# Pacing the loads of an opening stage: at most three on the way

## The chip, the cores and the metric

The kernel runs on one core of a Trainium2 chip. The metric is the time of one execution on the device in microseconds (us); lower is better. Before the change it is 587.9 us, the median of three runs (587.0 to 588.2).

## The reference

Two blocks follow each other. The first is a retention block: for each of 4 batches and 8 heads a 64 by 64 state decays by a factor of the head at each of 768 steps and takes in an outer product of k and v; the output at a step is q times the state. The second is a feed-forward layer on the result.

```python
for t in range(S):                      # S = 768; B, H, D = 4, 8, 64
    state = gamma[None, :, None, None] * state + np.einsum('bhd,bhe->bhde', k[:, :, t], v[:, :, t])
    y[:, :, t] = scale * np.einsum('bhd,bhde->bhe', q[:, :, t], state)
x = y.transpose(0, 2, 1, 3).reshape(B * S, H * D)      # 3072 x 512
h = x @ w_in                                           # 512 x 2048
g = h * (1.0 / (1.0 + np.exp(-h)))
out = g @ w_out                                        # 2048 x 512
```

The weights w_in and w_out come as 64-bit floating point, everything else as 32-bit.

## The kernel before

The sequence is cut into chunks of 128 steps, 6 for each batch. A pair of a chunk and a batch is a *unit*; there are 24, counted chunk by chunk (units 0 to 3 are the four batches of chunk 0). For a unit the kernel

- loads its k, q and v, 256 KB each (`load`, one DMA of 1024 runs of 256 bytes, issued by SyncE),
- transposes k and q on PE (`T`, or `TK` and `TQ` apart) and copies them out of PSUM with ACT,
- scales k and q on DVE by the decay (`K`, `Q`; `KA` does it on ACT),
- makes the scores and the state's increments on PE (`SC`, which reads k, v and the transposes), masks them on DVE (`A`),
- makes the unit's y on PE (`YS`, `Y0`, `YB`) and splits it into three parts for the exact products with w_in (`X`).

The weights are converted from 64 bits and split in the same way. A *slice* of w_in is 128 of its 2048 columns: `load_w` brings it in three DMAs, one of 256 KB and two of 128 KB, into one of two buffers (`wf`), and ACT and DVE convert and split it in small steps (`W`). When a chunk's y is there, PE multiplies it with the slices (`PP`, `PH`, and `product_in` later); g goes to DRAM and comes back for the product with w_out, which fills the second half of the kernel.

The order of the work up to the first products is **written out by hand** for all engines, SyncE's DMA issues among them: a long list of calls at the end of the function, from `load("k", 0)` down to `begin_w()`, closed by `early_order.close()`. After that only PE's order is written; the other engines, SyncE too, are placed by the scheduler. SyncE issues in order, so an issue that waits holds all later ones. What an issue waits for before the change is a free buffer (for a load into a buffer that was used before) and, for the DMA lanes, of which there are eight, the landing of the eighth DMA ahead of it.

`hold(done)` writes a SyncE instruction that does nothing but wait until the instruction `done` is complete, for a DMA until it has landed. Before the change nothing calls it.

Of the kernel before, what the change touches and what calls it, by code (L numbers as in the profile page):

```python
# [35 lines left out]
def kernel(  # L36
# [28 lines left out]
    nc = tc.nc  # L65
    B, H, S, D = q.shape
    DM, DF = moe_w_in.shape
    C = 128
# [64 lines left out]
    def split_w(*of):  # L133
        steps = split_steps(*of)
        next(steps)
        yield
        list(steps)
# [15 lines left out]
    early, last = {}, []  # L153

    def load(name, n):
        if n >= len(units):
            return
        c, b = units[n]
        src = {"k": k, "q": q, "v": v}[name]
        if n == 4 * B and name == "k":  # L160
            t = conv.tile([128, H, D], FP32, tag="wl", name=f"kf_{n}")
            nc.sync.dma_start(out=t, in_=src[b, :, ds(c * C, C)].rearrange("h t d -> t h d"))
            kqv[name][n] = t
            return
        if n < EARLY:

            if n not in early:
                early[n] = wpool.tile([128, 3, H, D], FP32, tag=f"w{4 + n}", name=f"kqv_{n}")
            t = early[n][:, "kqv".index(name)]
        else:  # L170
            t = ld.tile([128, H, D], FP32, tag=f"{name}f", name=f"{name}f_{n}",
                        bufs=2 if name == "q" else 3)
        nc.sync.dma_start(out=t, in_=src[b, :, ds(c * C, C)].rearrange("h t d -> t h d"))  # L173
        kqv[name][n] = t

    staged = {}

    def load_w(i):
        if i >= 2 * NF:
            return
        if wide:
            t = stage.tile([128, 2 * DM], U32, tag="wf", name=f"wf_{i}")
            w_in, w_out, n = moe_w_in.bitcast(U32), moe_w_out.bitcast(U32), 256
        else:
            t = stage.tile([128, DM], FP32, tag="wf", name=f"wf_{i}")
            w_in, w_out, n = moe_w_in, moe_w_out, 128
        if i < NF:  # L190
            to = t.rearrange("p (i o f) -> o p i f", o=2, f=n)
            src = w_in[:, ts(i, n)].rearrange("(i o p) f -> o p i f", o=2, p=128)
            last[:] = [nc.sync.dma_start(out=to[0], in_=src[0]).ins]
            for j in range(2):
                nc.sync.dma_start(out=to[1, ts(j, D)], in_=src[1, ts(1 - j, D)])
        else:
            nc.sync.dma_start(out=t, in_=w_out[ts(i - NF, 128), :])
        staged[i] = t
# [35 lines left out]
    def convert_w(i):  # L234

        if patient[0]:
            waiting.append(i + W_AHEAD)
        elif i + W_AHEAD not in staged:
            load_w(i + W_AHEAD)
        out = []  # L240
        steps = convert_steps(i, out)
        for _ in range(6):
            next(steps, None)

        def rounded():
            list(steps)
            return out[0]

        return rounded

    def early_slice(i):

        out = []
        yield from convert_steps(i, out)
        yield
        steps = split_steps(i, out[0], "wi", w_sb, None)
        next(steps)
        yield from steps
# [44 lines left out]
    def begin_w():  # L303

        i = taken[0]
        taken[0] += 1
        split = split_w(i, convert_w(i)(), "wi", w_sb, True)
        next(split)
        half_split.append(split)
# [102 lines left out]
    def hold(done):  # L412

        i = nc.sync.nop().ins
        tc.add_manual_dep(i, done.name, mybir.DependencyInfo(
            mybir.DependencyClass.Sync, mybir.DependencyReason.DATA), reason="hold")
# [276 lines left out]
    def halves(m):  # L693
# [36 lines left out]
        for name in "kqv":  # L730
            for n in (m + 1, m + 2):
                if (n, name) not in apart and EARLY <= n <= LATER and n == (
                        m + 1 if name == "v" or n >= LATER else m + 2):
                    load(name, n)
# [153 lines left out]
    def TQ(n):  # L888
        next(tsteps[n])
# [20 lines left out]
    def W(i, times=1):  # L910
        if i not in slices:
            slices[i] = early_slice(i)
        for _ in range(times):
            next(slices[i], None)

    def loads(n):
        for name in "kqv":
            load(name, n)
# [42 lines left out]
    def KA(n):  # L961
        t = kqv["k"][n]
        for h in range(H):
            nc.scalar.activation(out=t[:, h, :], in_=t[:, h, :], func=AF.Copy,
                                 scale=gk[:, units[n][0], h : h + 1])


    load("k", 0)
    load("q", 0)
    load("v", 0)  # L970
    load_w(0)
    load("k", 1)
    load("q", 1)
# [5 lines left out]
    load("q", 3)  # L979
    load("v", 3)  # L980
    load_w(1)
    load("k", 4)
    load("q", 4)
# [83 lines left out]
    X(3)  # L1067
    TQ(4)
    W(1)
    load("k",6)  # L1070
    W(1)
    load_w(2)
# [129 lines left out]
    Q(8)  # L1202
    load("q",11)
    taken[0] = 3
    begin_w()

    early_order.close()
# [9 lines left out]
    last = ([(c, f) for c in range(2) for f in range(NF - 4, NF)] +  # L1217
            [(2, f) for f in range(half, NF)])
# [84 lines left out]
    def apart_cols(t):  # L1303

        return t.rearrange("p (o n) -> p o n", o=2)

    def unwoven(t):

        return t.rearrange("p (n o) -> p o n", o=2)
# [8 lines left out]
    for c in range(NC):  # L1318
# [9 lines left out]
        for f in range(NF):  # L1328
# [4 lines left out]
            t = ready[n]  # L1333
            if f >= early_f:
                continue
            for b in range(B):
                gh, glo, gm = (t[:, i, ts(b, C)] for i in range(3))
                oa, ob = acc[b]
                for o, g, i in (oa, gh, 0), (oa, glo, 1), (ob, gm, 2):
                    nc.tensor.matmul(o, lhsT=g, rhs=woven(wo[f][:, i, :],  # L1340
                                                          (c, b) == (NC - 1, B - 1)),
                                     start=f == 0 and i != 1,
# [4 lines left out]
        if early_f < NF:  # L1347
# [3 lines left out]
                         for x in ("left", "right")]  # L1351
            nc.scalar.activation(out=apart_cols(halves_of[0]),
                                 in_=unwoven(acc[B - 1][0][:, left]), func=AF.Copy,
# [7 lines left out]
        for b, o, parts, cols in ends:  # L1361
            for f in range(early_f, NF):
                for i in parts:
# [3 lines left out]
                                     start=o is last_left and (f, i) == (early_f, 0),  # L1367
                                     stop=f == NF - 1 and i != 0,
                                     skip_group_check=cols != whole)
        for b in range(B):  # L1370
            oa, ob = acc[b]
            if c == NC - 1 and b == B - 1:
# [4 lines left out]
                for i, (x, cols, op) in enumerate(((last_left, left, ALU.add),  # L1377
                                                   (oa, right, ALU.subtract))):
                    nc.vector.scalar_tensor_tensor(
                        out=apart_cols(o[i]), in0=unwoven(x[:, cols]), scalar=ONE_E,  # L1380
# [44 lines left out]
```

## Time and profile before

| | before |
|---|---|
| median of three runs | 587.9 us |
| profiled execution | 586.4 us |
| its span, first to last instruction | 584.4 us |
| PE busy | 576.4 us, 99% of the span |
| DVE, ACT busy | 399.1 us, 321.7 us |
| DMA, mean over the span | 186 GB/s |

The profile is taken from one execution, which has its own time; the span lies inside that time. PE is the matrix engine, PEld its weight loads, DVE the vector engine, ACT the activation engine, POOL the general one, and SP is SyncE (SPq: its DMA issues). In rows of the timeline the columns are start, duration, engine, line, operation, and the tiles written and read. A row that begins with an engine and has an arrow and a name after it, such as "PE y L576 <- issue", tells who waited for whom: total us, times, longest. A tile view gives, for the instructions chosen, the shortest, median and longest duration in ns, the first and last start, and, for DMA issues, the time from the start of the issue to the landing. Buffer numbers are left out of the names: kqv holds k, q or v of units 0 to 7, kf, qf and vf those of later units, and wf a slice of the weights.

### The profile page before, as it was taken

Reading aid. Unit: us, or ns where it says so; the run is one execution under the profiler, and the core shown is the slowest. Engines: PE = TensorE matmul, PEld = TensorE weight load, DVE = VectorE, ACT = ScalarE, POOL = GpSimd, SP = SyncE. Lnnn points to the kernel's source line nnn. Section 1 sums busy time; section 2 is a strip of 40 time slices with the busy share of each in tenths; the row PEclk is TensorE's granted clock in tenths of the full one; section 3 lists DMA queues with packets and bytes.
Section 4 is the critical chain, followed back from the end, with each engine's and each line's share of the span. In section 5 each row is a group of like instructions: output and inputs, shape, how many; then the busy total and the mean of one; then the engine's idle time right before and its main releaser. Section 6 shows DMA issues by size and latency. Waiting matters only on the chain.

```text
span 584.4 us, 13651 instructions
## 1 busy us (share of the span) xinstructions
PE 576.4 (99%) x5512; PEld 499.9 (86%) x5512; DVE 399.1 (68%) x678; ACT 321.7 (55%) x561; POOL 29.4 (5%) x84
## 2 busy tenths in 40 slices
PE   8999999999999999999999999999999999999997
PEld 6787888888888888888888888888888888888886
DVE  3898998678678876666799994736545563645632
ACT  7657766546356466545566675544544545545311
POOL 3000000100031211210000000000000000000000
PEclk9999999999999999999999999999999999999999
DMA  9998978986489899997589862523524443433301
GB/s 193 215 220 192 218 192 278 267 259 214 145 192 232 234 283 284 255 265 230 171 281 326 288 207 77 195 93 111 178 79 139 144 119 97 165 123 102 115 1 72
DMA packets 144334, 108.89 MB, mean 186 GB/s; under 512 B 101136, under 2 KB 109584, under 8 KB 144272
## 3 DMA queue, kind: packets, MB, share of 16 engines
q1 hardware_dynamic: 144128, 107.90, 66.0%
q8 instruction: 43, 0.70, 0.5%
q14 instruction: 19, 0.16, 0.1%
q10 hardware_dynamic: 144, 0.13, 0.1%
HBM read 66.06 MB, written 36.70 MB: 176 GB/s over the span
## 4 chain that ended last, share of the span: by engine, by line
PE 95%; SPq 2%; DVE 1%; DMA 1%; issue 1%; ACT 0%; DVEq 0%; POOL 0%; POOLq 0%; ACTq 0%
PE ha L757 28%; PE o L1340 21%; PE oa L1340 14%; PE hb L757 14%; PE ob L1340 7%; PE y L576 4%; PE sc L518 2%; PE sc L528 2%; SPq L173 1%; DMA kqv<-in_q_dram 1%; PE ha L928 1%; PE kp L486 1%; PE qp L486 0%; PE o L1364 0%; PE hb L928 0%
## 5 line engine op out<-in xcount | busy, mean ns | idle before, releaser
L757 PE MATMUL ha<-xt,wi 128*128 128x512 f32 x736 | 175.7, 382 | 0.0
L757 PEld LDWEIGHTS ha<-xt,wi 128*128 128x128 f32 x736 | 137.7, 189 | 20.0
L1340 PE MATMUL o<-wo,gs 128*128 128x512 f32 x564 | 137.2, 379 | 0.0
L1340 PEld LDWEIGHTS o<-wo,gs 128*128 128x128 f32 x564 | 106.5, 189 | 15.3 <-DVE o L1389 0.2
L852 DVE TENSOR_TENSOR gs<-gr,gs 128x512 fp32r<-128x512 f32 x96 | 62.0, 684 | 83.0 <-ACT gs L850 83.0
L1340 PE MATMUL oa<-wo,gs 128*128 128x512 f32 x376 | 111.8, 379 | 0.0
L849 ACT ACTIVATE gr<-gr 128x512 f32<-128x512 f32 x96 | 59.7, 629 | 67.8 <-DMA gr<-gd 63.8
L757 PE MATMUL hb<-xt,wi 128*128 128x512 f32 x368 | 94.4, 379 | 0.0
L781 ACT ACTIVATE g<-ha 128x512 f32<-128x512 f32 x87 | 52.1, 599 | 76.5 <-PE ha L757 64.9
L787 DVE SCALAR_TENSOR_TENSOR g<-hb,g 128x512 f32<-128x512 f32 x87 | 59.7, 686 | 40.5 <-ACT g L781 33.6
L1340 PEld LDWEIGHTS oa<-wo,gs 128*128 128x128 f32 x376 | 71.1, 189 | 10.1
L757 PEld LDWEIGHTS hb<-xt,wi 128*128 128x128 f32 x368 | 69.6, 189 | 9.9
L850 ACT ACTIVATE gs<-gr 128x512 fp32r<-128x512 f32 x96 | 53.1, 621 | 38.7 <-PE ob L1340 30.4
L1340 PE MATMUL ob<-wo,gs 128*128 128x512 f32 x188 | 71.3, 379 | 0.0
L853 DVE SCALAR_TENSOR_TENSOR gs<-gs 128x512 fp32r<-128x512 f32 x96 | 61.9, 682 | 0.1
L1340 PEld LDWEIGHTS ob<-wo,gs 128*128 128x128 f32 x188 | 35.5, 189 | 5.1
L212 ACT ACTIVATE ca<-wf 128x512 f32<-128x512 f32 x32 | 27.1, 847 | 15.1 <-DVE cs L225 9.1
L225 DVE SCALAR_TENSOR_TENSOR cs<-ca,cs 128x512 uint32<-128x512 uint32 x32 | 22.1, 690 | 0.8
L536 DVE TENSOR_TENSOR am<-sc,decay 128x512 f32<-128x512 f32 x24 | 16.5, 686 | 8.8 <-PE sc L528 7.7
L576 PE MATMUL y<-qt,mid 64*64 64x64 f32 x376 | 20.0, 220 | 0.9 <-issue 0.9
L657 DVE SCALAR_TENSOR_TENSOR xt<-xt 128x512 fp32r<-128x512 f32 x28 | 19.6, 704 | 0.5
L1389 DVE TENSOR_TENSOR o<-o,o 128x512 f32<-128x512 f32 x10 | 6.6, 687 | 17.8 <-ACT o L1388 17.8
(137 smaller groups left out, 582.9 us busy)
## 6 DMA issues: line engine op xcount, KB each, us to landing
gr<-gd SPq DMA_DIRECT2D x96, 256.0 KB, 2.8
gd<-g SPq DMA_DIRECT2D x87, 256.0 KB, 3.8
wf<-in_moe_w_out_dram SPq DMA_DIRECT2D x16, 512.0 KB, 4.4
out_dram<-o SPq DMA_DIRECT2D x23, 256.0 KB, 2.4
wf<-in_moe_w_in_dram SPq DMA_DIRECT2D x16, 256.0 KB, 4.4
wf<-in_moe_w_in_dram SPq DMA_DIRECT2D x32, 128.0 KB, 4.2
kf<-in_k_dram SPq DMA_DIRECT2D x16, 256.0 KB, 4.6
qf<-in_q_dram SPq DMA_DIRECT2D x16, 256.0 KB, 4.4
```

Source lines behind the costliest of these rows:

```text
L212: top = nc.scalar.activation(out=a.bitcast(FP32), in_=hi.bitcast(FP32), func=AF.Abs, scale=2.0 ** -3).ins
L225: nc.vector.scalar_tensor_tensor(out=s, in0=a, scalar=3, in1=s, op0=ALU.logical_shift_left, op1=ALU.bitwise_xor)
L576: i = nc.tensor.matmul(to[ts(e, D), o, a, :], lhsT=lhsT, rhs=rhs, start=key not in started, stop=True, skip_group_check=True).ins
L657: nc.vector.scalar_tensor_tensor(out=x[2], in0=x[1].bitcast(FP32), scalar=-1.0 / EPS, in1=x[0].bitcast(FP32), op0=ALU.mult, op1=ALU.add)
L757: nc.tensor.matmul(hb if i == 2 else ha, lhsT=w_sb[f][:, i, ts(kk, 128)], rhs=woven(xt[c][:, i, kk, :]), start=kk == 0 and i != 1, stop=kk ...
L781: copied[:] = [nc.scalar.activation(out=to, in_=ha, func=AF.Copy, scale=scale * ONE_E).ins]
L787: taken_out[:] = [nc.vector.scalar_tensor_tensor(out=to, in0=hb, scalar=-scale, in1=to, op0=ALU.mult, op1=ALU.add).ins]
L849: nc.scalar.activation(out=g, in_=g, func=AF.Silu)
L850: nc.scalar.activation(out=t[:, 0, :], in_=g, func=AF.Copy, scale=HALF)
L852: nc.vector.tensor_tensor(out=t[:, 1, :], in0=g, in1=high, op=ALU.subtract)
L853: nc.vector.scalar_tensor_tensor(out=t[:, 2, :], in0=t[:, 1, :].bitcast(FP32), scalar=-1.0 / EPS, in1=high, op0=ALU.mult, op1=ALU.add)
L1340: nc.tensor.matmul(o, lhsT=g, rhs=woven(wo[f][:, i, :], (c, b) == (NC - 1, B - 1)), start=f == 0 and i != 1, stop=f == NF - 1 and i != 0 o ...
```

## The change

From unit 6's k in the written order to the end of that order, SyncE issues a load only when the third load ahead of it has landed. All loads of `load` and the w_in loads of `load_w` go through a new function `paced`, which keeps a list of them and, while `pace[0]` is not zero, calls `hold` on the third last. Pacing is turned on just before `load("k",6)` and off just before `begin_w()`. Each of the three DMAs of a slice counts as a load.

```diff
-        nc.sync.dma_start(out=t, in_=src[b, :, ds(c * C, C)].rearrange("h t d -> t h d"))
+        paced(nc.sync.dma_start, out=t, in_=src[b, :, ds(c * C, C)].rearrange("h t d -> t h d"))
...
+    flying, pace = [], [0]
+
+    def paced(start, **operands):
+        if pace[0] and len(flying) >= pace[0]:
+            hold(flying[-pace[0]])
+        flying.append(start(**operands).ins)
+        return flying[-1]
...
-            last[:] = [nc.sync.dma_start(out=to[0], in_=src[0]).ins]
+            last[:] = [paced(nc.sync.dma_start, out=to[0], in_=src[0])]
             for j in range(2):
-                nc.sync.dma_start(out=to[1, ts(j, D)], in_=src[1, ts(1 - j, D)])
+                paced(nc.sync.dma_start, out=to[1, ts(j, D)], in_=src[1, ts(1 - j, D)])
...
     W(1)
+    pace[0] = 3
     load("k",6)
...
     taken[0] = 3
+    pace[0] = 0
     begin_w()
```

The order of the instructions stays the same on every engine; only what SyncE waits for changes. Before, at the start of the stretch, SyncE's issues and the semaphores that each waits for are these (DMAHW0 to DMAHW7 are the eight lanes; the first rows are q and v of unit 5, then unit 6's k, the third slice's three pieces, unit 6's q, unit 7's k, unit 6's v).

```order
L173 DMA kqv_308<-in_q_dram 128x8x64 [waits DMAHW6_49]
L173 DMA kqv_308<-in_v_dram 128x8x64 [waits DMAHW7_49]
L173 DMA kqv_821<-in_k_dram 128x8x64 [waits DMAHW0_49]
L193 DMA wf_823<-in_moe_w_in_dram 128x2x256 [waits DMAHW1_49,DVE_49,Activation_49]
L195 DMA wf_823<-in_moe_w_in_dram 64x2x256 [waits DMAHW2_49]
L195 DMA wf_823<-in_moe_w_in_dram 64x2x256 [waits DMAHW3_49]
L173 DMA kqv_821<-in_q_dram 128x8x64 [waits DMAHW4_49]
L173 DMA kqv_828<-in_k_dram 128x8x64 [waits DMAHW5_49]
L173 DMA kqv_821<-in_v_dram 128x8x64 [waits DMAHW6_49]
```

Each waits for its own lane, that is for the eighth DMA ahead of it. The same issues after the change:

```order
L181 DMA kqv_308<-in_q_dram 128x8x64 [waits DMAHW6_49]
L181 DMA kqv_308<-in_v_dram 128x8x64 [waits DMAHW7_49]
L181 DMA kqv_821<-in_k_dram 128x8x64 [waits DMAHW5_49,DMAHW0_49]
L181 DMA wf_824<-in_moe_w_in_dram 128x2x256 [waits DVE_49,DMAHW1_49,DMAHW6_49,Activation_49]
L181 DMA wf_824<-in_moe_w_in_dram 64x2x256 [waits DMAHW7_49,DMAHW2_49]
L181 DMA wf_824<-in_moe_w_in_dram 64x2x256 [waits DMAHW0_49,DMAHW3_49]
L181 DMA kqv_821<-in_q_dram 128x8x64 [waits DMAHW1_49,DMAHW4_49]
L181 DMA kqv_833<-in_k_dram 128x8x64 [waits DMAHW2_49,DMAHW5_49]
L181 DMA kqv_821<-in_v_dram 128x8x64 [waits DMAHW3_49,DMAHW6_49]
```

From unit 6's k on each issue waits for one lane more, that of the third load ahead: unit 6's q (lanes 1 and 4) for the slice's main piece, which went out on lane 1, and unit 6's v (lanes 3 and 6) for the slice's last piece on lane 3. 26 issues have such a wait, the last being that of unit 11's q.

## The prediction

> **What bounds the kernel now.** First the page: the span, the share of each engine, and the chain that ended last.
>
> ```profile
> span 584.4 us, 13651 instructions
> PE 576.4 (99%) x5512; PEld 499.9 (86%) x5512; DVE 399.1 (68%) x678; ACT 321.7 (55%) x561; POOL 29.4 (5%) x84
> PE 95%; SPq 2%; DVE 1%; DMA 1%; issue 1%; ACT 0%; DVEq 0%; POOL 0%; POOLq 0%; ACTq 0%
> ```
>
> PE is the bound from end to end: 576.4 of 584.4 us. PE's order is written by hand, and it is the same in both kernels, so a microsecond that PE waits is a microsecond of the end, and a load that lands sooner than PE wants it is worth nothing. The question is therefore how much PE waits in the stretch that the change touches. Next the table by stretches, for the paced stretch (26 to 57 us) and what follows, and the chain, for the last place where it runs through a load.
>
> ```profile
> 26.00:57.00 31.00, 29.66 (x684) 25.16 (x685) 27.16 (x50) 20.70 (x44) 0.36 (x4) 1.00 1.00 217
> 57.00:75.00 18.00, 18.00 (x401) 15.15 (x400) 17.72 (x34) 11.64 (x26) 0.27 (x3) 1.00 0.86 195
> 10.47 4.75 DMA kqv<-in_q_dram
> ```
>
> The columns of the first two rows are the stretch, its length, the busy time of PE, PEld, DVE, ACT and POOL, the granted clock, the DMA share and GB/s. PE idles 31.00 - 29.66 = 1.34 us in the paced stretch and not at all in the next. The clock is 1.00 in both. The last load in the chain is a unit's q that lands at 15.2 us; from there on PE, DVE and ACT set the pace although the DMA engines are full (share 1.00). So the kernel gains nothing by loads that come sooner, and the price of the change is how far it eats into the lead that the loads have over PE.
>
> **What the change does to the queue.** No instruction moves on any engine. Of SyncE's loads, 26 get one more wait: unit 6's k, six q, five more k, five v, and nine pieces of three w_in slices (a slice is a piece of 256 KB and two of 128 KB, and each piece counts as a load). Today SyncE runs ahead as far as the queue takes it:
>
> ```profile
> 26.16 0.82 SPq L173 DMA_DIRECT2D kqv<-in_k_dram  x1
> 27.11 1.21 SPq L193 DMA_DIRECT2D wf<-in_moe_w_in_dram  x1
> 28.37 1.26 SPq L195 DMA_DIRECT2D wf<-in_moe_w_in_dram  x2
> 29.67 0.60 SPq L173 DMA_DIRECT2D kqv<-in_q_dram  x1
> 30.32 1.11 SPq L173 DMA_DIRECT2D kqv<-in_k_dram  x1
> 31.48 2.22 SPq L173 DMA_DIRECT2D kqv<-in_v_dram  x1
> 53.92 0.82 SPq L173 DMA_DIRECT2D qf<-in_q_dram  x1
> ```
>
> These are the issues of unit 6's k, the third w_in slice, unit 6's q, unit 7's k, unit 6's v, and, last of the paced ones, unit 11's q. The tile view in a narrow window gives the landing of a single load, counted from the start of its issue; in the order of the rows: unit 6's k, the slice's main piece, one of its small pieces, unit 6's q, its v, unit 11's q.
>
> ```profile
> L173 SPq DMA_DIRECT2D kqv<-in_k_dram x1: 822/822/822, 26.2 to 26.2; - x1
> DMA to landing us min/median/max: 4.8/4.8/4.8
> ...
> L193 SPq DMA_DIRECT2D wf<-in_moe_w_in_dram x1: 1211/1211/1211, 27.1 to 27.1; - x1
> DMA to landing us min/median/max: 5.9/5.9/5.9
> ...
> L195 SPq DMA_DIRECT2D wf<-in_moe_w_in_dram x1: 609/609/609, 29.0 to 29.0; - x1
> DMA to landing us min/median/max: 5.4/5.4/5.4
> ...
> L173 SPq DMA_DIRECT2D kqv<-in_q_dram x1: 603/603/603, 29.7 to 29.7; - x1
> DMA to landing us min/median/max: 5.5/5.5/5.5
> ...
> L173 SPq DMA_DIRECT2D kqv<-in_v_dram x1: 2221/2221/2221, 31.5 to 31.5; - x1
> DMA to landing us min/median/max: 5.6/5.6/5.6
> ...
> L173 SPq DMA_DIRECT2D qf<-in_q_dram x1: 824/824/824, 53.9 to 53.9; - x1
> DMA to landing us min/median/max: 4.7/4.7/4.7
> ```
>
> Unit 6's k lands at 26.16 + 4.8 = 31.0, unit 11's q, 25 loads later, at 53.92 + 4.7 = 58.6: 27.6 us, or 1.1 us a load. An issue to landing of about 5.3 us at 1.1 us a load means that four to five loads are under way at a time. The change leaves at most three. What three can carry depends on how long one load takes with less before it. The nearest row is a load of the same size later on, with the queue almost empty:
>
> ```profile
> L162 SPq DMA_DIRECT2D kf<-in_k_dram x1: 387/387/387, 156.8 to 156.8; - x1
> DMA to landing us min/median/max: 3.1/3.1/3.1
> ```
>
> With 0.1 us for SyncE to see the landing and start (an estimate: its own gaps between issues in the rows above are 0.04 to 0.13), three loads in 3.1 + 0.1 us are 1.07 us a load, which is what the full queue delivers now, 1.1. That is the lower bound of the new pace. The upper bound is today's 5.3 us to landing: 5.4 / 3 = 1.8 us a load. I take a value near the lower end, about 1.2, because most of today's 5.3 us is time behind the loads ahead, and there will be fewer of them. It is not 1.07 because the six small pieces now hold a place among the three for as long as a whole load, where today they pass in about half its time: 6 times 0.5 us is some 3 us over the stretch.
>
> The Trainium skill, page "DMA: Bandwidth & Descriptors", section "Anatomy of one DMA — SWDGE (gpsimd) path", puts a transfer at 2.0 us and its bytes over 436 GB/s. By that a 256 KB load would take an estimated 2.6 us, three in flight would give 0.9 us a load, and pacing would cost nothing at all; the 3.1 us of the row above are longer, and the measurement decides.
>
> **Where PE meets a late load.** The leads are smallest where pacing begins, just behind the w_in slice. The rows are PE's transposes of unit 6's q, its products with unit 6's v, and the transposes of unit 11's q.
>
> ```profile
> 36.40 0.60 PE L486 MATMUL qp<-ident,kqv 128*128 128x128 f32 x4
> ...
> 38.81 0.34 PE L518 MATMUL sc<-kqv 64*64 64x64 f32 x8
> ...
> 63.38 0.22 PE L496 MATMUL kp<-ident,qf 64*128 64x64 f32 x1
> ```
>
> Unit 6's q lands at 29.67 + 5.5 = 35.2, so it leads by 1.2 us. Now it waits for the third load ahead, the slice's main piece, which lands at 27.11 + 5.9 = 33.0. That piece stands behind the same loads as before, so I keep its landing. The q then starts at 33.1 and lands at the earliest at 33.1 + 3.1 = 36.2, just in time; by today's 5.5 us it would be 38.6, 2.2 us late. Between them I take one other load's 1.1 us in front of it: 37.3, which is 0.9 us late. Unit 6's v waits for the small piece, 29.02 + 5.4 = 34.4 (its issue starts 0.65 us behind the first small piece's). It starts at 34.5, earliest landing 37.6, with two loads in front of it about 39.3, against 38.81: 0.5 late, but PE has already slipped 0.9, so that adds nothing. For unit 11's q, 25 loads at 1.2 us instead of 1.1 put it 2.5 us later, at 61.1 against 63.38: still in time. The slips don't add up, since PE is moved once by the latest of them.
>
> Everything else is covered. The added waits themselves (a SyncE wait instruction takes hundredths of a microsecond) stand where SyncE would wait anyway. Behind the waiting SyncE are only the later loads of the written order, then the next w_in slices and the stores, which are due later still; their cover is the same lead that unit 11's q has, several times the slip. If it were gone, a late w_in slice would stop ACT and DVE, which convert it, for as long as it is late. The sum: -0.1 to +2.2 us, taken as +0.8, the 0.9 less 0.1 for a PE idle moment that falls into the slip.
>
> **The rivals.** (1) Pacing hides entirely: the load takes its unhurried 3.1 us, q lands at 36.2, v at 37.6 or a little behind, and PE never waits. For it: 1.07 against 1.1 us a load. Against: the lead left is 0.2 us at one place. Time: that of before, give or take 0.2.
>
> (2) Faster: with a shorter queue, the short transfers that compete with the loads (instructions for the engines among them) come through sooner and PE's small stops go. These are PE's largest waits from 26 to 64 us (total, times, longest):
>
> ```profile
> PE y L576 <- issue: 0.9, 2, 0.6
> PE sc L518 <- issue: 0.3, 1, 0.3
> PE y L576 <- POOL token L407: 0.3, 1, 0.3
> ```
>
> The two kinds that nothing in the trace explains ("issue") are 1.2 us together. With all of PE's idle time gone the gain is 1.34 us; I take 0.6. The profile does not say that the queue causes these stops. The same page of the Trainium skill, section "Queues, rings and completion order", says that each DMA engine takes turns between the queues that have work, a packet at a time; by that a transfer on another queue doesn't wait behind all loads, a shorter queue would save it little, and this rival would give nothing. No row here shows the turns.
>
> (3) Slower: three in flight don't fill the DMA engines. The mechanism is SyncE's round trip: a landing, then an issue, then the flight. Its place is the far end of the paced stretch, where the lags of 25 loads have added up. The lead of unit 11's q is 63.38 - 58.6 = 4.8 us, so it decides from 27.6 + 4.8 = 32.4 us for 25 loads, 1.3 us a load, an issue to landing of 3.8 us. Halfway between 3.1 and 5.3, at 4.2 us, a load comes every 1.43 us, 25 take 35.8, unit 11's q lands at 66.8 and PE waits 3.4 us there. At 4.0 us to landing it would be 1.8 us, at 4.5 us 5.9. For it: a landing takes as much as 5.9 us here. Against: those were behind four others.
>
> **How the numbers follow.** The profiled execution took 586.4 us, its span 584.4, some 2 us lying outside; the median of the three runs is 587.9, and I add to that. My forecast, a slip of 0.2 to 2.2 us at unit 6, has 0.42 and gives 587.9 + 0.8 = 588.7, at most 590.1. The hidden case has 0.24 (587.9), the faster 0.18 (587.3, at best 586.6), the slower 0.16 (591.3, from 589.7 to 593.8). A measurement of this kernel can tell about 0.2% from no change, 1.2 us. Beyond that lie, on the slow side, all of the last case and some 0.15 of the first, 0.31 together; on the fast side half of the faster case, 0.09; the remaining 0.60 is within. The range 586.6 to 590.8 takes in the bounds of the first three cases and the beginning of the slower one.
>
> **What would show it.** Right: in the profile after, the loads from unit 6's k on take 3.1 to 4.2 us to land, not 5.3; PE or PEld has a new wait of 0.5 to 1 us put down to a load of q or v at 36 to 39 us, and unit 11's q still comes in time. The hidden case shows no such wait and 29.7 us of PE in the same 31. The faster case shows fewer "issue" waits. The slower one shows PE waiting for a load near 58 to 65 us. The forecast is wrong if PE waits more than 2 us for loads, or if the time moves while no wait for a load appears.

## The result and the profile after

The changed kernel takes 589.8 us, the median of nine runs (588.3 to 592.0), against 587.9 us (587.0 to 588.2) before: a ratio of 1.0038, 95% interval 1.0026 to 1.0051. By the ratio it is some 2.2 us slower, by the medians 1.9. The forecast of 588.7 us was too low by about 1 us; the range held. Two executions of the variants below ran at a granted clock of 0.85 and 0.75, the profiled one with four in flight among them, and no time or row here comes from them.

The first rows are the page of the profile after, its span, engines and the chain that ended last; the next two are the same stretches as in the prediction, 26 to 57 and 57 to 75 us, now with pacing.

```profile
span 588.1 us, 13676 instructions
PE 575.9 (98%) x5512; PEld 499.0 (85%) x5512; DVE 400.3 (68%) x678; ACT 321.5 (55%) x561; POOL 28.9 (5%) x84
PE 87%; DMA 7%; SPq 4%; issue 0%; ACT 0%; DVE 0%; DVEq 0%; ACTq 0%
...
26.00:57.00 31.00, 28.34 (x682) 24.17 (x683) 27.01 (x50) 19.99 (x43) 0.35 (x4) 1.00 0.80 183
57.00:75.00 18.00, 17.05 (x394) 14.04 (x393) 16.64 (x32) 11.76 (x26) 0.18 (x2) 1.00 0.90 209
```

PE does the same work (575.9 us) in a longer span. DMA and SyncE had 1% and 2% of the chain and have 7% and 4%. In the paced stretch the DMA engines fell from a share of 1.00 and 217 GB/s to 0.80 and 183: on average a fifth of them now stands idle, while SyncE waits for landings. PE idles 2.7 us there instead of 1.3, and 0.95 us in the next stretch, where it had no idle time. The two profiled spans differ by 3.7 us, more than the medians; 1.3 us of that are two later stalls of PE, which come up again below.

These are PE's waits from 26 to 80 us (total, times, longest):

```profile
PE qp L492 <- DMA kqv<-in_q_dram: 1.1, 1, 1.1
PE sc L524 <- DMA kqv<-in_v_dram: 0.7, 1, 0.7
PE kp L502 <- DMA qf<-in_q_dram: 0.6, 2, 0.4
PE sc L524 <- DVE kqv L430: 0.4, 1, 0.4
PE kp L502 <- DMA kf<-in_k_dram: 0.4, 1, 0.4
...
PE y L582 <- issue: 0.2, 1, 0.2
```

The loads waited for are unit 6's q and v and, behind 57 us, the q of units 10 and 11 and unit 11's k. Together these waits are 2.8 us, where the profile of before had none in this stretch. "issue" is down from 1.2 us to 0.2. It may be that stops which PE had anyway have gone into the waits, but that is not shown: such stops vary from none to 1.5 us in the profiles below. The same three PE rows as in the prediction, now, in the timeline:

```profile
37.50 0.52 PE L492 MATMUL qp<-ident,kqv 128*128 128x128 f32 x3 [1.06 <-DMA kqv<-in_q_dram]
...
40.54 0.35 PE L524 MATMUL sc<-kqv 64*64 64x64 f32 x9 [0.69 <-DMA kqv<-in_v_dram]
...
65.26 0.27 PE L502 MATMUL kp<-ident,qf 64*128 64x64 f32 x1 [0.22 <-DMA qf<-in_q_dram]
```

They were at 36.40, 38.81 and 63.38 us: 1.1, 1.7 and 1.9 us late. How the loads came to be late is read off the chain of waits, in order of time (start, duration, what):

```profile
27.73 4.42 DMA kqv<-in_k_dram
...
32.16 0.02 SPq L420
...
32.21 3.19 DMA wf<-in_moe_w_in_dram
...
35.42 0.02 SPq L420
...
35.47 4.94 DMA kqv<-in_v_dram
...
40.54 0.69 PE sc L524 x32
```

Unit 6's k goes out at 27.73 and takes 4.42 us; L420, the new wait (the line of `hold`), ends 0.03 us after it landed and the slice's last piece starts 0.03 us later; that piece, half as large, takes 3.19 us; then unit 6's v takes 4.94 us, and PE starts on it. Up to PE the chain is nothing but flights, one after the other, with 0.06 to 0.07 us between them.

### The profile page after: what moved, and what is told of

Its sections match the earlier page's. It is cut to its first block, busy times and chain, and to the rows that moved or that the text cites. A ratio compares the mean times of both kernels' runs of the same rounds, so it can differ in the third digit from the quotient of the medians.

```text
span 588.1 us, 13676 instructions
## 1 busy us (share of the span) xinstructions
PE 575.9 (98%) x5512; PEld 499.0 (85%) x5512; DVE 400.3 (68%) x678; ACT 321.5 (55%) x561; POOL 28.9 (5%) x84
## 4 chain that ended last, share of the span: by engine, by line
PE 87%; DMA 7%; SPq 4%; issue 0%; ACT 0%; DVE 0%; DVEq 0%; ACTq 0%
PE ha L763 26%; PE o L1348 21%; PE oa L1348 14%; PE hb L763 12%; PE ob L1348 7%; SPq L181 4%; PE y L582 3%; DMA wf<-in_moe_w_in_dram 2%; DMA kqv<-in_k_dram 2%; PE sc L524 1%; PE sc L534 1%; DMA wf<-in_moe_w_out_dram 1%; DMA kqv<-in_v_dram 1%; DMA qf<-in_q_dram 1%; DMA wr<-wod 1%; DMA vf<-in_v_dram 1%
```

## The experiments

Two explanations stood against each other at first: the supply is limited by the round trip of a load divided by the number in flight; or the wait instructions themselves, or something later in the kernel, cost the time. All runs below are the changed kernel with the edit shown, compared with the kernel before on the same chip. Losses in us are worked out from the ratios; the medians give up to 0.4 us more or less.

**Two in flight.**

```diff
-    pace[0] = 3
+    pace[0] = 2
```

> Pace 2 instead of 3: an issue waits for the second load ahead. Theory (a load's round trip, some 3.1 to 4.3 us from issue to landing in the run with pace 3, divided by the number in flight, sets the supply): two in flight give 1.6 to 2.1 us a load, 25 loads take 40 to 52 us instead of 27.6, the leads of 1.2 to 4.8 us are gone many times over, and the kernel is 8 to 14 us slower than before. Rival A (the added wait instructions are what costs, not what they wait for): same count of waits as with pace 3, so +2 us as there. Rival B (the loss lies later, in stalls near 84 and 324 us that have nothing to do with loads): +2 us as there.

598.3 us against 585.9: ratio 1.0207 (1.0191 to 1.0223), 12.1 us slower. PE's waits for loads from 26 to 80 us, and the issue to landing of the paced loads (the last number, median us):

```profile
PE kp L502 <- DMA qf<-in_q_dram: 5.4, 2, 4.2
PE sc L524 <- DMA kqv<-in_v_dram: 1.9, 2, 1.3
PE qp L492 <- DMA kqv<-in_q_dram: 1.8, 1, 1.8
PE sc L524 <- DMA vf<-in_v_dram: 1.6, 1, 1.6
...
kf<-in_k_dram SPq DMA_DIRECT2D x4, 256.0 KB, 3.3
qf<-in_q_dram SPq DMA_DIRECT2D x4, 256.0 KB, 3.1
wf<-in_moe_w_in_dram SPq DMA_DIRECT2D x6, 128.0 KB, 3.3
```

A single load lands sooner than with three in flight, after 3.0 to 3.5 us by kind, and half a load (128 KB) takes as long as a whole one. Two of them in 3.3 + 0.06 us are 1.7 us a load. The same count of wait instructions cost some six times as much, so it is what they wait for. The waits for loads are 10.7 us of the 12.1. Some of the rest may be the clock: the granted clock from 57 to 75 us was 0.91 in this execution, 1.00 before.

**Four in flight.**

```diff
-    pace[0] = 3
+    pace[0] = 4
```

> Pace 4: an issue waits for the fourth load ahead. Theory: four in flight at a round trip of 3.1 to 4.3 us give 0.8 to 1.1 us a load, which is what the full queue delivered before, so no load is late: 0 to +0.3 us against before, and PE waits for no load behind 30 us. Rival A (wait instructions): +2 us, as with pace 3. Rival B (later stalls): +2 us or as it happens.

586.6 against 585.9 us: ratio 1.0011 (0.9998 to 1.0023). One more in flight takes nearly all of the loss away. What is left, 0.6 us, can't be told from nothing, and which waits it is made of is not shown here.

**Waits that are over already.**

```diff
-    pace[0] = 3
+    pace[0] = 8
```

> Pace 8: the same 26 wait instructions, each for the eighth load ahead, which SyncE waits for anyway before it can use the DMA lane again. Theory: 0 within 0.2 us against before. Rival A (the wait instructions cost by themselves): +1 to +2 us.

585.7 against 585.9 us, ratio 0.9997 (0.9986 to 1.0009): the added wait instructions by themselves cost nothing that these runs can tell. The profile has 21 of them as separate instructions on L420, as many as that of the changed kernel.

**The slices neither wait nor count.**

```diff
-            last[:] = [paced(nc.sync.dma_start, out=to[0], in_=src[0])]
+            last[:] = [nc.sync.dma_start(out=to[0], in_=src[0]).ins]
             for j in range(2):
-                paced(nc.sync.dma_start, out=to[1, ts(j, D)], in_=src[1, ts(1 - j, D)])
+                nc.sync.dma_start(out=to[1, ts(j, D)], in_=src[1, ts(1 - j, D)])
```

> Pace 3, but the nine pieces of the three w_in slices neither wait nor count among the three. Theory (the slice's pieces, two of them half as large, hold places in the queue of three just ahead of unit 6's q and v): q and v of unit 6 then wait for q and k of unit 5 and 6 that landed earlier, they land as early as before, and the kernel is within 0.4 us of before. Rival C (three in flight are too few whatever is counted): unit 6's q is in time but k and q of unit 11 are late as with pace 3, +1 us.

586.0 against 585.9 us, ratio 1.0001 (0.9989 to 1.0013). PE waits for no load; its waits from 26 us to the end are

```profile
PE y L582 <- issue: 1.5, 3, 0.8
PE y L582 <- POOL token L413: 0.3, 1, 0.3
PE y L582 <- DVE qt L435: 0.2, 1, 0.2
```

So three of k, q and v in flight are enough when the slices go beside them, and rival C falls. The transfers on the way are then more than three whenever a slice passes.

**A slice counts once.** Only the two small pieces are taken out; the main piece waits and counts.

```diff
             for j in range(2):
-                paced(nc.sync.dma_start, out=to[1, ts(j, D)], in_=src[1, ts(1 - j, D)])
+                nc.sync.dma_start(out=to[1, ts(j, D)], in_=src[1, ts(1 - j, D)])
```

> Pace 3, but a w_in slice counts as one load: its main piece of 256 KB waits and counts, its two small pieces of 128 KB go out right behind it without a wait. Theory (a small piece takes as long from issue to landing as a whole one, so with a place of its own it costs a whole turn): 19 turns instead of 25 from unit 6's k to unit 11's q at 1.3 us each are 25 us, less than the 27.6 us of before, so no load is late: within 0.2% of before, and no wait of PE for a load behind 30 us. Rival (the main pieces alone already fill the three places): +1 us or more, with waits for q and v of unit 6 as in the changed kernel.

585.8 against 586.3 us, ratio 0.9990 (0.9978 to 1.0003). PE's waits from 15 us to the end are

```profile
PE y L582 <- issue: 0.9, 2, 0.5
PE y L582 <- POOL token L413: 0.3, 1, 0.3
PE qp L492 <- DMA kqv<-in_q_dram: 0.2, 1, 0.2
PE sc L524 <- DVE kqv L430: 0.2, 1, 0.2
PE y L582 <- DVE qt L435: 0.2, 1, 0.2
```

The one wait for a load ends at 15.4 us, ahead of the paced stretch; behind 30 us there is none, as expected, and the time is that of before. Taking away the places of the six half-size loads is enough to take away the whole loss. That isn't quite the same as the pieces being its only cause, since without places of their own more transfers are on the way as well, and a fourth place for all loads did nearly as much.

**The first part alone, the second part alone.** For the first part alone, pacing is turned off from unit 8's k on:

```diff
     load("v",7)
     A(4)
+    pace[0] = 0
     load("k",8)
```

For the second part alone, it is turned on only there:

```diff
-    pace[0] = 3
     load("k",6)
...
     A(4)
+    pace[0] = 3
     load("k",8)
```

> Pace 3 only from unit 6's k to unit 7's v, off from unit 8's k on. Theory (two places: unit 6's q and v behind the slice, then unit 11's k and q at the far end): only the first is left. In the run with pace 3 throughout, PE is 1.7 us late behind unit 6's v and some 1.0 us late at 57 us, because stops that it has anyway fall into the waits. So +0.6 to +1.2 us against before, and no wait for a load of q10, k11 or q11. Rival (the whole loss comes from unit 6): +2 us, as with pace 3 throughout.

> Pace 3 only from unit 8's k to unit 11's q. Theory (the lag of a load grows by some 0.25 us a load; 16 loads make 4 us, and unit 11's q leads by 4.8 us): q just comes in time, 0 to +0.4 us. Rival D (the far end alone makes the loss, because the latest slip sets the end): +1.5 to +2 us, as with pace 3 throughout.

The first part: 587.5 against 586.4 us, ratio 1.0017 (1.0006 to 1.0027), 1.0 us. The second: 586.3, ratio 1.0000 (0.9988 to 1.0012). PE's waits for loads, in the first and then in the second:

```profile
PE sc L524 <- DMA kqv<-in_v_dram: 1.0, 1, 1.0
PE qp L492 <- DMA kqv<-in_q_dram: 0.2, 1, 0.2
...
PE kp L502 <- DMA qf<-in_q_dram: 0.2, 1, 0.2
```

Both as expected. In its profile, which comes from the fastest of its twelve executions, the second part alone uses up the far end's whole lead: unit 11's q is 0.2 us late, and the time shows no loss. That it loses behind the lag which the first part has already made is an inference from the changed kernel, where both parts are paced.

**The changed kernel again.**

> The changed kernel again, on the same chip as the three others. Theory: +2 us, of which 1.5 to 2 us are waits of PE for loads; the stall of 0.8 us near 324 us behind a load of w_out, in the first profile of it, does not come again if it has nothing to do with the change. Rival B (the later stalls belong to it): both come again.

587.7 against 586.4 us: ratio 1.0029 (1.0017 to 1.0042), so 1.7 us here. The profile is from one of the two fastest of its ten executions, 586.6 us, which is hardly longer than the median of before, so it shows only part of the loss. This time unit 6's q and v came in time, and the far end was late:

```profile
PE kp L502 <- DMA qf<-in_q_dram: 0.7, 2, 0.4
...
PE kp L502 <- DMA kf<-in_k_dram: 0.2, 1, 0.2
```

The waits for loads are 0.9 us in this execution, less than the 1.5 to 2 that were expected, and 2.8 in the first. The leads at unit 6 are so small that the two profiled executions fall on either side of them. The first profile of the changed kernel had two more stalls of PE later on, of 0.5 us at 84 us and of 0.8 us at 324 us; here neither came, so they are not a fixed part of the change. What makes them stays open: a stall of the second kind, of 0.6 us, is also in the profile of the first part alone.

**Unit 6's q and v ahead of the slice.**

```diff
     load("k",6)
     W(1)
+    load("q",6)
+    load("v",6)
     load_w(2)
-    load("q",6)
     load("k",7)
     W(1)
     W(1)
-    load("v",6)
     load("q",7)
```

> Pace 3 throughout, but unit 6's q and v are issued ahead of the third w_in slice instead of behind it. Theory: q then waits for unit 5's q and v for unit 5's v, both land by 34 us, and PE's waits for q and v of unit 6 go. The loads behind stay as late as before, since as many of them pass the queue; unit 11's q still lands near 65 us against a need of 63.4 us. Because the latest slip sets the end, the kernel keeps +1.2 to +2.0 us. Rival (the loss is made at unit 6 alone): within 0.4 us of before.

588.2 against 586.4 us, ratio 1.0033 (1.0021 to 1.0045). The time is as expected, the way there only in part. PE's waits from 26 to 80 us, and what DVE waited for just before:

```profile
PE sc L524 <- DVE kqv L430: 1.6, 2, 1.1
PE y L582 <- issue: 1.5, 1, 1.5
...
PE kp L502 <- DMA qf<-in_q_dram: 0.2, 1, 0.2
...
36.31 0.55 DVE L221 TENSOR_SCALAR cs<-wf 128x512 uint32<-128x512 uint32 x1 [0.55 <-DMA wf<-in_moe_w_in_dram]
37.20 0.43 DVE L227 TENSOR_SCALAR ca<-ca 128x512 f32<-128x512 f32 x1 [0.35 <-ACT ca L218]
```

The waits for unit 6's q and v are gone, as the theory has it. But now the slice is late: DVE, which works in the written order, stands 0.9 us at its conversion, and the scaling of unit 6's k behind it makes PE wait 1.1 us. Together with a stop of 1.5 us of another kind in this execution ("issue"), little is left for the far end, 0.2 us. Moving the late place doesn't help while the supply is short; whether the far end alone would have made the same loss, this run doesn't say.

No version is faster than before; four in flight, or a slice that counts once, cost nothing that these runs can tell.

## Why the prediction was right, and where it was off

*The forecast as a whole.* The time fell within the range, 1.1 us above the forecast, but two of the forecast's own signs speak against its path. PE waited 2.8 us for loads in the first profile, where more than 2 was to mean that the forecast is wrong, and unit 11's q, which was to be in time, was late in both profiles. The path, one slip at unit 6 with the supply keeping pace behind it, is therefore only half of what happened. That its number still came near the measured one is in part luck: what it left out added about 1 us.

*PE is the bound, so loads matter only where they come too late.* Right: PE's busy time is the same within 0.5 us, and each variant without a wait for a load has the time of before.

*Unit 6's q waits for the slice's main piece, is issued at 33.1, lands at 37.3, and PE is 0.9 us late.* It was issued at 33.02, landed 4.3 us later at 37.3, and PE was 1.1 us late in the first profile; in the second it came in time. The range for this term, -0.1 to +2.2 us, held both.

*Unit 6's v adds nothing.* Wrong in the first profile: 0.7 us more. The landing of the slice's last piece was kept at 34.4 us. It landed at 35.4, because it now waited for unit 6's k, which had itself waited for unit 5's k and so went out at 27.73 us instead of 26.16. The step that failed is the assumption that a piece ahead keeps its landing: the added waits pass a lag on from third load to third load. The sum for v had a slip of its own: 37.6 and two loads at 1.1 us each are 39.8, not 39.3, which is 1.0 us late and no longer quite covered by the 0.9 of q. In the second profile v came in time, as q did.

*1.2 us a load, so unit 11's q lands at 61.1 and leads.* Mis-sized. From the landing of unit 6's k (32.1) to that of unit 11's q (60.89 + 4.3 = 65.2) it was 33.1 us for 25 loads, 1.32 a load. It was 1.32 in the second profile too (31.0 to 63.8). Between the issues of these two loads, the timelines give 1.1 us a load before, with eight in the count and with a slice that counts once, 1.0 with slices that don't count, 1.3 with three in flight and 1.7 with two. The loss follows this pace. The issue to landing with three in flight was not near the unhurried 3.1 us:

```profile
kf<-in_k_dram SPq DMA_DIRECT2D x4, 256.0 KB, 4.0
qf<-in_q_dram SPq DMA_DIRECT2D x4, 256.0 KB, 4.2
kqv<-in_v_dram SPq DMA_DIRECT2D x3, 256.0 KB, 4.5
wf<-in_moe_w_in_dram SPq DMA_DIRECT2D x6, 128.0 KB, 3.2
vf<-in_v_dram SPq DMA_DIRECT2D x3, 256.0 KB, 3.8
```

At some 4.0 us, (4.0 + 0.06) / 3 = 1.35 us a load. That crosses the 1.3 us from which the third rival decides, but barely. Its place (the far end) was right, and its price of 3.4 us, which was for 4.2 us to landing, too high. The 1.8 us that it gave for 4.0 us to landing are near the 1.9 us by which PE came late to unit 11's q in the first profile. The waits there are only 0.9 to 1.0 us in the two profiles; in the first, PE was 1.0 us late already at 50 us. The result is the forecast and the beginning of that rival together. The first rival, that pacing hides entirely, falls: both intervals of the changed kernel lie above 1.

*The small pieces hold a place for as long as a whole load.* Nearly so with three in flight, 3.2 us for half the bytes against 3.8 to 4.5 for a whole load, and fully so with two. It weighs more than the prediction made of it, since taking just these six out of the count takes the whole loss away.

*The second rival (faster, by fewer stops of PE).* Not borne out. The queue was shorter in two variants without a late load: issue to landing was 4.0 to 5.0 us by kind with slices that don't count and 3.9 to 4.9 with a slice that counts once, against 4.9 to 5.7 before. Their "issue" stops from 26 to 80 us are 1.5 and 0.4 us against 1.2 before, and both intervals of their times take in 1.

The Trainium skill, page "DMA: Bandwidth & Descriptors", section "Anatomy of one DMA — SWDGE (gpsimd) path", gives 2.0 us plus bytes over 436 GB/s, an estimated 2.6 us for 256 KB and 2.3 us for 128 KB; that section is on DMAs that GpSimd issues, and these are issued by SyncE. The trace agrees that size counts for little (3.0 to 3.5 us and 3.3 us with two in flight), but not with the level, and by the level pacing at three would have been free.

## What to carry to other kernels

A limit on the loads in flight sets the time between loads at the round trip divided by that number; measure the round trip at that depth. Where small transfers share the queue, don't give each a place of its own: here a slice that counted once cost nothing. A limit counted in bytes was not tried. Compare the time between loads with the lead that the consumer has left at the end of the stretch, not only at its start, and let each lag pass on through the waits instead of keeping the landings of before. Where the engine that bounds the kernel never waits for a load, a shorter queue has little to win; no variant here was faster.

## What the runs showed of the hardware

With two in flight a load of 128 KB took as long as one of 256 KB (3.3 us against 3.0 to 3.5 by kind); with three it took 3.2 us against 3.8 to 4.5 in the same profile. The round trip of a 256 KB load grew with the number in flight, from about 3.3 us at two to 4.0 and more at three (3.8 to 4.8 by kind in two profiles) and about 5.3 (5.1 to 5.7 by kind) with the queue full. With SyncE waiting, the next issue started 0.06 to 0.07 us after a landing. Two loads in flight moved 150 GB/s in the paced stretch, three 183, the full queue 217.
